# Token sums from stored halves, on GpSimd, during attention; rows of y in places of their own; second halves of weights at new paces

## The chip, the cores and the metric

The kernel runs on one core of a Trainium2 chip, in one launch. The time is the device time of that core in microseconds (us). The kernel before took a median of 1056.4 us over three runs (1053.79 to 1057.5).

## The reference

What is computed is random-feature attention, a gated feed-forward layer, and a second feed-forward layer with a cosine gate, all in fp32:

```python
q_p, k_p = phi(q_s), phi(k_s)             # exp features, 128 of them
kv = np.einsum('bhsm,bhsd->bhmd', k_p, v)
num = np.einsum('bhsm,bhmd->bhsd', q_p, kv)
den = np.einsum('bhsm,bhm->bhs', q_p, k_p.sum(axis=2))[..., None] + 1e-06
x = (num / den), as 2304 tokens x 512
# layer 1: 512 -> 1536 -> 512
xn = x / rms * rms_g
g = xn @ w_gate
x = (g / (1 + exp(-g)) * (xn @ w_val)) @ w_out
# layer 2: 512 -> 2048 -> 512
h = x @ w_in
out = (h * np.cos(h)) @ w_out2
```

4 batches, 8 heads, 576 positions, head size 64. The weights arrive as float64.

## The kernel before, in words

**Tiling.** The 2304 tokens are 18 tiles of 128, or 6 blocks of 384; two blocks that follow each other are a pair, so there are 3 pairs. The 1536 hidden features of layer 1 are 12 chunks in three groups of four, the 2048 of layer 2 are 16 chunks in groups of 6, 5 and 5. Every fp32 operand of a matmul is kept as a high and a low half of type fp32r, and a product is three matmul passes (high x high, low x high, high x low).

**Weights.** The class `Weights` turns each 128x512 chunk of float64 into fp32 on the device: that is its front (`front`: four VectorE instructions on lines 165, 167, 169 and 174, one ScalarE scaling on L159, one GpSimd add on L177). The result goes to DRAM (`keep`, tensors `kept`), comes back later (`ask`, tile `b`), and is split in two halves (`split`: a ScalarE cast on L182 and a GpSimd subtraction on L185): that is its back, the second half of its way. The first 12 chunks are split straight after their front. Fronts and backs are generators: `pace` takes so many steps of each at a rate that `rate` and `rate_back` work out from the steps left, and `get` runs them at once where a product needs a chunk that isn't there. In `ask` (L203) a back that finds its chunk not yet stored runs fronts on the spot until it is.

**Attention and the first group.** 24 slots project keys and the first six query tiles. Then 48 half steps run the first group of layer 1 (gate and value product of one chunk for one block: tile `gv_ps`, 12 matmuls; output product into `y_ps`) with the steps of the twelve query tiles that remain woven in: per tile, a projection, exponentials, two transposes, the sums, the root mean square (`root`, L443 and L444 on GpSimd), the scaling (`norm`, L448 on VectorE), a transpose on TensorE (`turn`, L458, tile `xT_ps`) and the split into `xhl`. A block's halves are stored to `x_dram` when done.

**Pairs.** Groups two and three of layer 1 use a scheme with seven block products for a pair instead of eight. It needs combinations of the two blocks' token sums, T1 to T4, made once per pair by the generator `combinations` from the halves still in SBUF: 8 sums on VectorE (L561), 16 subtractions on GpSimd (L565), 8 casts on ScalarE (L569), and their stores. `job` steps it during the half steps; for the third pair what is left is run with `job(99)` in the last half step. `bring` loads operands for a pair (tiles `B` and `T`, 768 KB each). In the stretch of pairs `duo` makes the seven products (tiles X and Y, line 986, with ScalarE copies on L1011 and VectorE additions on L1014 to L1029), `ys` the output product (L1065). `unit` is the beat there: every six or so matmuls it runs what is due, one flushed job, and paced steps of weights. Partial sums of y are kept in `y_dram`; `ask(g, blk, e)` loads one row of 192 KB again and `add_y` adds to it.

**Layer 2.** `hidden` and `h_cos` make a step (12 matmuls `h_ps`, then ScalarE and VectorE), `out2` the output product two steps later (36 matmuls `o_ps`).

**What sets the order.** Each engine works its instructions in the order in which the program makes them, and SyncE (SP) issues nearly all transfers in its own such order: a transfer that waits holds back all behind it. TensorE's instructions are the same, in the same order, before and after the change.

## Time and profile before

| | |
|---|---|
| median of 3 runs | 1056.4 us |
| profiled execution: time, span | 1059.7 us, 1057.9 us |
| TensorE matmuls, busy | 990.3 us (94%) |
| VectorE, busy | 726.8 us (69%) |
| ScalarE, busy | 520.2 us (49%) |
| GpSimd, busy | 331.2 us (31%) |
| DMA queue of SP, share of 16 engines | 49.0% |

Busy time is an average over stretches that differ: attention with the first group (up to 331 us), the pairs (331 to 655 us) and layer 2 (to the end, where TensorE has no gap worth naming). TensorE is the engine that everything ends on, so what counts is where it stood idle and what it waited for, and where its clock was granted at the lower of its two levels after such a wait.

### The profile page before, as it was taken

The page shows a single profiled execution, that of the slowest core. Times are in us where ns is not written, and L with a number is a line of the kernel's source. Part 1 is how long each engine was busy: PE and PEld are TensorE (multiplying, and loading weights), DVE is VectorE, ACT ScalarE, POOL GpSimd, SP SyncE. Part 2 cuts the span into 40 slices and gives each one's busy share as a digit, 9 for nine tenths or more (in the row PEclk, how much of TensorE's full clock was granted, in tenths as well). Part 3 has the DMA queues.
Part 4 walks back from the last instruction along what each step waited for, and adds up shares of the span by engine and source line. Part 5 has one row for each costly group of instructions (what it writes and reads, how often), then busy time and mean ns, then how long its engine had stood idle before and what let it go on. Part 6 is the DMA issues. An engine that isn't in the chain of part 4 may idle for free.

```text
span 1057.9 us, 16240 instructions
## 1 busy us (share of the span) xinstructions
PE 990.3 (94%) x5905; PEld 931.6 (88%) x5905; DVE 726.8 (69%) x1275; ACT 520.2 (49%) x1133; POOL 331.2 (31%) x293
## 2 busy tenths in 40 slices
PE   9999599999986899999899986999999999999998
PEld 7988589999986798999899986999999999999997
DVE  6788897788743667687677676877555676656555
ACT  6777476776422524253534443545444444443442
POOL 2143456246255543375824274121100111000000
PEclk9999889999998899999999998999999999999999
DMA  8554464645477487846898787433301223103401
GB/s 292 151 167 164 138 209 161 209 164 178 148 255 275 149 338 250 316 123 217 297 329 301 263 288 260 158 132 128 140 1 64 96 90 129 60 1 117 152 31 60
DMA packets 75295, 185.15 MB, mean 175 GB/s; under 512 B 8016, under 2 KB 32720, under 8 KB 75216
## 3 DMA queue, kind: packets, MB, share of 16 engines
q1 hardware_dynamic: 73776, 179.34, 49.0%
q10 hardware_dynamic: 1440, 4.78, 1.3%
q8 instruction: 46, 0.75, 0.3%
q14 instruction: 33, 0.27, 0.1%
HBM read 126.94 MB, written 57.15 MB: 174 GB/s over the span
## 4 chain that ended last, share of the span: by engine, by line
PE 68%; DMA 13%; DVE 8%; issue 3%; POOL 3%; ACT 2%; SPq 1%; ACTq 0%; POOLq 0%; DVEq 0%
PE h_ps L738 18%; PE o_ps L731 6%; PE o_ps L732 6%; PE gv_ps L738 6%; PE o_ps L730 6%; PE X L986 5%; PE Y L986 4%; PE y_ps L802 4%; DMA b<-kept 3%; PE y L1065 3%; DMA y<-y_dram 3%; PE num_ps L420 2%; DMA kept<-f 2%; PE kv_ps L531 2%; DMA y_dram<-y 2%
## 5 line engine op out<-in xcount | busy, mean ns | idle before, releaser
L738 PE MATMUL h_ps<-yhl,w 128*128 128x384 f32 x1152 | 217.2, 337 | 0.0
L738 PEld LDWEIGHTS h_ps<-yhl,w 128*128 128x128 f32 x1152 | 204.9, 188 | 8.2
L177 POOL TENSOR_TENSOR f<-f,raw 128x512 f32<-128x512 f32 x68 | 94.3, 1387 | 258.9 <-DVE raw L174 231.0
L185 POOL TENSOR_TENSOR w<-b,w 128x512 fp32r<-128x512 f32 x72 | 96.5, 1347 | 186.4 <-ACT w L182 101.4
L730 PE MATMUL o_ps<-w,o 128*128 128x512 f32 x288 | 112.8, 392 | 9.3 <-ACT o L827 9.3
L732 PE MATMUL o_ps<-w,o 128*128 128x512 f32 x288 | 114.6, 398 | 0.0
L731 PE MATMUL o_ps<-w,o 128*128 128x512 f32 x288 | 114.4, 397 | 0.0
L824 ACT ACTIVATE turns<-turns,half_pi 128x384 f32<-128x384 f32 x96 | 59.2, 617 | 108.6 <-DVE turns L819 108.6
L1065 PE MATMUL y<-t,w 128*128 128x384 f32 x576 | 104.5, 341 | 7.0 <-ACT t L994 7.0
L738 PE MATMUL gv_ps<-xhl,w 128*128 128x384 f32 x576 | 109.2, 338 | 0.8 <-DVE eT L410 0.4
L1065 PEld LDWEIGHTS y<-t,w 128*128 128x128 f32 x576 | 102.8, 193 | 7.7 <-ACT t L994 7.7
L738 PEld LDWEIGHTS gv_ps<-xhl,w 128*128 128x128 f32 x576 | 101.8, 190 | 1.6 <-DVE eT L410 1.0
L986 PE MATMUL X<-T,w 128*128 128x384 f32 x432 | 83.6, 341 | 10.7 <-ACT r L1011 8.7
L829 DVE TENSOR_TENSOR o<-turns,o 128x384 fp32r<-128x384 f32 x96 | 55.1, 574 | 51.8 <-ACT o L827 51.2
L986 PEld LDWEIGHTS X<-T,w 128*128 128x128 f32 x432 | 76.8, 192 | 12.1 <-ACT r L1011 9.8
L826 DVE TENSOR_TENSOR turns<-h_ps,turns 128x384 f32<-128x384 f32 x96 | 53.4, 556 | 46.8 <-ACT turns L824 46.3
L827 ACT CAST o<-turns 128x384 fp32r<-128x384 f32 x96 | 49.3, 513 | 67.9 <-DVE turns L826 67.3
L818 DVE SCALAR_TENSOR_TENSOR r<-turns,h_ps 128x384 f32<-128x384 int32 x96 | 53.1, 554 | 36.2 <-ACT turns L817 36.1
L802 PE MATMUL y_ps<-t,w 128*128 128x384 f32 x288 | 62.8, 354 | 10.9 <-ACT t L789 8.6
L817 ACT ACTIVATE turns<-h_ps,quarter 128x384 int32<-128x384 f32 x96 | 55.7, 580 | 34.4 <-PE h_ps L738 34.0
L730 PEld LDWEIGHTS o_ps<-w,o 128*128 128x128 f32 x288 | 54.5, 189 | 18.4 <-ACT o L827 9.6
L182 ACT CAST w<-b 128x512 fp32r<-128x512 f32 x72 | 42.6, 597 | 46.5 <-DMA b<-kept 36.3
(102 smaller groups left out, 1767.0 us busy)
## 6 DMA issues: line engine op xcount, KB each, us to landing
raw<-wc SPq DMA_DIRECT2D x59, 512.0 KB, 4.2
yhl<-yh_dram SPq DMA_DIRECT2D x32, 768.0 KB, 5.9
T<-T_dram SPq DMA_DIRECT2D x20, 768.0 KB, 9.3
kept<-f SPq DMA_DIRECT2D x56, 256.0 KB, 4.5
b<-kept SPq DMA_DIRECT2D x56, 256.0 KB, 3.7
B<-x_dram SPq DMA_DIRECT2D x15, 768.0 KB, 7.2
x_dram<-xhl SPq DMA_DIRECT2D x12, 768.0 KB, 6.1
y_dram<-y SPq DMA_DIRECT2D x48, 192.0 KB, 2.4
```

The costliest lines, as they stand in the source:

```text
L177: nc.gpsimd.tensor_tensor(f32(f), f32(f), rest, op=ALU.add)
L185: nc.gpsimd.tensor_tensor(t[:, 1, to], src, f32(t[:, 0, to]), op=ALU.subtract)
L730: nc.tensor.matmul(o, w[0], x[0], start=first, stop=False)
L731: nc.tensor.matmul(o, w[0], x[1], start=False, stop=False)
L732: nc.tensor.matmul(o, w[1], x[0], start=False, stop=last)
L738: nc.tensor.matmul(o, w[i], x[j], start=n == 0, stop=n == len(terms) - 1)
L802: nc.tensor.matmul(yacc[blk][e], w[:, i, e * P:(e + 1) * P], t[:, j], start=first and i + j == 0, stop=last and j == 1)
L817: nc.scalar.activation(a, h, AF.Identity, bias=quarter, scale=1.0 / (2 * math.pi))
L824: nc.scalar.activation(r, r, AF.Sin, bias=half_pi)
L829: nc.vector.tensor_tensor(o[:, 1], r, f32(o[:, 0]), op=ALU.subtract)
L986: nc.tensor.matmul(o, w[:, i, c + kk * P:c + (kk + 1) * P], x[:, j, kk], start=begin and n == 0, stop=n == 5, skip_group_check=True)
L1065: nc.tensor.matmul(acc[e], w[:, i, e * P:(e + 1) * P], t[:, j], start=f == fs[0] and i + j == 0, stop=f == fs[-1] and j == 1)
```

## The change

Six edits go together.

1. **Token sums.** `combinations` no longer reads the halves in SBUF. It loads high and low half of each operand again from `x_dram` into one tile (`ask`, four loads for each half of a pair), and makes the sums with GpSimd (L585), as it does the subtractions (L588, L597). The high halves are a GpSimd copy too (L594) for the first two pairs, a ScalarE copy (L592) for the third. High and low half stand in one tile and are stored with one transfer; they stand in reverse order, which `seventh` takes into account.
2. **The third pair's sums** move out of the first group: `limit` stops `job` after two pairs, and `unit` steps the third pair's sums during the stretch of pairs. `bring` puts off the load of a T that isn't made yet. `job(99)` is gone.
3. **Rows of y** that `put_away` stores at the end of the first group, and those that `ask` loads again, have a tag of their own with 7 buffers, where they shared four buffers with the hidden rows or had four. The rows of the second block of a pair are asked for during `duo`, all but the last. Their additions, and the store after them, come a unit or more later.
4. **Fronts** load two chunks ahead from within the front instead of three ahead after its end. A back no longer runs fronts when its chunk isn't stored: it gives way (`BLOCKED`), unless `get` forces it. The tile `b` has four buffers, and the chunk after next is asked for earlier.
5. **Paces.** 32 chunks (before: 25) have their front by the end of the first group, 54 (before: 56) by the start of layer 2. Backs don't start before six fronts are done, then run at 1.0 or 1.3 steps a unit among pairs. The last fronts are spread over 52 steps of layer 2 instead of 32.
6. **Room.** One buffer of weights less in the first ring (20), two in the second; fewer buffers for loads and features of attention once the keys are done.

```diff
         def ask(self, c):
-            if c < len(self.todo) and c not in self.b:
-                while c not in self.kept:
-                    next(self.fronts)
-                b = self.b[c] = conv.tile([P, 512], F32, tag="b", name=f"b{c}", bufs=3)
+            if c in self.kept and c not in self.b:
+                b = self.b[c] = conv.tile([P, 512], F32, tag="b", name=f"b{c}", bufs=4)
                 nc.sync.dma_start(b, self.kept[c])
...
         def back(self, c):
+            while c not in self.kept:
+                if not self.forced:
+                    yield BLOCKED
+                else:
+                    next(self.fronts)
+                    self.n_front += 1
             self.ask(c)
             self.ask(c + 1)
...
             g, v = self.b.pop(c - 1), self.b.pop(c)
+            self.ask(c + 2)
...
-        jobs = []
+        jobs, combined, limit = [], set(), [NPAIR - 1]
...
-            def total(x, kk, name):
-                r = tp.tile([P, NB], F32, tag="r", name=f"{name}_{p}_{kk}")
-                nc.vector.tensor_tensor(r, f32(x[:, 0, kk]), f32(x[:, 1, kk]), op=ALU.add)
-                return r
+            def ask(b, i, kk):
+                a = tp[0].tile([P, 2, NB], F32, tag="s", name=f"s{p}_{b}_{i}_{kk}", bufs=tp[1])
+                nc.sync.dma_start(a, in_dram[2 * p + b][i][:, :, kk])
+                return a
+
+            def total(a):
+                nc.gpsimd.tensor_tensor(a[:, 0], a[:, 0], a[:, 1], op=ALU.add)
...
+            def high(a):
+                if few:
+                    nc.scalar.copy(a[:, 1].bitcast(F32R), a[:, 0])
+                else:
+                    nc.gpsimd.tensor_copy(a[:, 1].bitcast(F32R), a[:, 0])
...
-            y = row(F32, f"y{blk}_{e}")
+            y = row(F32, f"y{blk}_{e}") if not more else more[0].tile([P, NB], F32, tag="y", name=f"y{blk}_{e}", bufs=YROWS)
...
         def bring(g, p, name):
+            if name[0] == "T" and p not in combined:
+                at(1, bring, g, p, name)
+                return
...
+        FRONTS_BY_1, FRONTS_BY_2 = 32, 54
...
-            rates = wts.rate(2 * C1 * G + 1, N1 - n) / 2, 1.0 if tail else wts.rate_back(C1 * G + 6, N1 - G - n) / 2
+            back = 2.0 if tail else wts.rate_back(C1 * G + 5, N1 - G - n) / 2
+            if wts.n_front < 6 * FRONT:
+                back = 0.0
+            rates = wts.rate(FRONTS_BY_1, N1 - G + 1 - n) / 2 if n <= N1 - G else 0.0, back
...
-            if n == N1 - 1:
-                job(99)
...
-            wts.pace(*tempo)
+            wts.pace(tempo[0] if clock[0] >= 30 else 0.0, 1.3 if clock[0] % (3 * UNITS) >= 100 or clock[0] % (3 * UNITS) < 16 else 1.0)
+            job(2 if clock[0] % 5 < 2 else 1)
...
                     if i < KD:
                         at(3, ask, g, 2 * p, i)
+                    elif i < 7:
+                        at(3, ask, g, 2 * p + 1, i - KD)
...
-            for e in range(KD):
-                at(3 + e, ask, g, 2 * p + 1, e)
+            at(6, ask, g, 2 * p + 1, 3)
```

VectorE in the fifth half step of the first group: `qmx7` belongs to query tile 7, `x5` is the row of tile 5 that `turn` waits for; `f12` to `f15` and `raw12` to `raw14` are fronts of weights. Before:

```order
L391 TENSOR_REDUCE qmx7_1_1579<-qp_ps7_1_1562 128x4
L174 SCALAR_TENSOR_TENSOR raw11_1315<-raw11_1315 128x512
L165 TENSOR_SCALAR f12_1598<-W12_1519 128x512
L167 SCALAR_TENSOR_TENSOR f12_1598<-W12_1519,f12_1598 128x512
L169 TENSOR_SCALAR raw12_1409<-f12_1598 128x512
L174 SCALAR_TENSOR_TENSOR raw12_1409<-raw12_1409 128x512
...
L165 TENSOR_SCALAR f15_1638<-W15_1632 128x512
L167 SCALAR_TENSOR_TENSOR f15_1638<-W15_1632,f15_1638 128x512
L448 SCALAR_TENSOR_TENSOR x5_1433<-x5_1433,ms5_1488,gain_255 128x512
L788 TENSOR_TENSOR gv0_2_1538<-gv_ps0_2_1_1646,gv0_2_1538 128x384
```

Now, in the same place:

```order
L399 TENSOR_REDUCE qmx7_1_1572<-qp_ps7_1_1555 128x4
L169 SCALAR_TENSOR_TENSOR f11_1508<-W11_1457,f11_1508 128x512
L171 TENSOR_SCALAR raw11_1315<-f11_1508 128x512
L456 SCALAR_TENSOR_TENSOR x5_1430<-x5_1430,ms5_1484,gain_255 128x512
L838 TENSOR_TENSOR gv0_2_1531<-gv_ps0_2_1_1590,gv0_2_1531 128x384
```

Fifteen instructions of fronts stood between the two rows of attention; now there are two.

GpSimd in half steps 26 to 28 of the first group: `b11` to `b22` (before) and `s1` (now) are the sums of the second pair, `ms14` is the root mean square of query tile 14. Before:

```order
L443 TENSOR_SCALAR ms13_2851<-ms13_2851 128x1
L444 TENSOR_TENSOR ms13_2851<-ms13_2851,minus_half_76 128x1
L565 TENSOR_TENSOR b21_1_0_2955<-b21_1_0_2955,b22_1_0_2824 128x384
L565 TENSOR_TENSOR b22_1_0_2824<-b22_1_0_2824,T2h_1_0_2946 128x384
L565 TENSOR_TENSOR b21_1_0_2955<-b21_1_0_2955,T4h_1_0_3012 128x384
L565 TENSOR_TENSOR b11_1_1_3072<-b12_1_1_3074,b11_1_1_3072 128x384
L443 TENSOR_SCALAR ms14_3048<-ms14_3048 128x1
```

Now:

```order
L588 TENSOR_TENSOR s1_1_0_0_2786<-s1_1_1_0_2796,s1_1_0_0_2786 128x384
L588 TENSOR_TENSOR s1_1_1_0_2796<-s1_1_1_0_2796,s1_0_0_0_2784 128x384
L594 CAST s1_0_0_0_2784<-s1_0_0_0_2784 128x384
L597 TENSOR_TENSOR s1_0_0_0_2784<-s1_0_0_0_2784 128x384
L594 CAST s1_1_0_0_2786<-s1_1_0_0_2786 128x384
L597 TENSOR_TENSOR s1_1_0_0_2786<-s1_1_0_0_2786 128x384
L183 TENSOR_TENSOR f23_2984<-f23_2984,raw23_2789 128x512
L191 TENSOR_TENSOR w14_2990<-b13_2470,w14_2990 128x512
L585 TENSOR_TENSOR s1_0_1_0_2831<-s1_0_1_0_2831 128x384
L588 TENSOR_TENSOR s1_0_1_0_2831<-s1_0_1_0_2831,s1_1_1_0_2796 128x384
L594 CAST s1_1_1_0_2796<-s1_1_1_0_2796 128x384
L451 TENSOR_SCALAR ms14_3021<-ms14_3021 128x1
```

Between the roots of tiles 13 and 14 stood four GpSimd instructions; now there are sixteen, of which these are the last eleven.

SP where the operands of the third pair come in (T1_1_2 to T4_1_2), now; before, each stood between single rows of y, without a store of T ahead:

```order
L1103 DMA y1_3_2_4820<-y_dram3_2_3435 128x384
L600 DMA T2_dram2_3954<-s2_1_1_1_4449 256x1x384
L600 DMA T4_dram2_3956<-s2_0_1_1_4672 256x1x384
L966 DMA T4_1_2_4847<-T4_dram2_3956 128x1536
L966 DMA T3_1_2_4849<-T3_dram2_3955 128x1536
L966 DMA T1_1_2_4851<-T1_dram2_3953 128x1536
L966 DMA T2_1_2_4853<-T2_dram2_3954 128x1536
```

The four loads follow the last stores of the sums at once, and T2, the first of them that TensorE uses, is the last in the queue.

## Rows read from the trace of the kernel before

**Rows 1.** Waits of PE: line, releaser: us in total, times, longest

```profile
PE xT_ps L458 <- DVE x L448: 11.8, 1, 11.8
PE o_ps L730 <- ACT o L827: 9.3, 1, 9.3
PE X L986 <- ACT r L1011: 8.7, 3, 4.7
PE y_ps L802 <- ACT t L789: 8.6, 1, 8.6
PE y L1065 <- ACT t L994: 7.0, 2, 3.9
PE Y L986 <- DVE r L1014: 4.9, 7, 2.0
PE y_ps L802 <- ACT y L768: 2.4, 1, 2.4
```

**Rows 2.** Windows: length, busy PE, PEld, DVE, ACT, POOL; PEclk, DMA share, GB/s

```profile
133.00:138.00 5.00, 4.75 (x20) 4.78 (x21) 4.35 (x8) 4.37 (x9) 2.09 (x2) 0.53 0.71 213
324.00:329.00 5.00, 4.54 (x14) 4.54 (x15) 1.16 (x2) 2.31 (x5) 4.36 (x5) 0.51 0.42 153
350.00:357.00 7.00, 6.20 (x21) 6.20 (x22) 2.62 (x5) 3.17 (x7) 2.74 (x3) 0.56 0.52 181
526.00:531.00 5.00, 4.85 (x19) 4.85 (x20) 2.71 (x3) 1.96 (x5) 4.49 (x5) 0.66 1.04 409
655.00:661.00 6.00, 5.13 (x16) 4.26 (x17) 4.70 (x10) 2.82 (x6) 1.29 (x1) 0.59 0.60 202
```

**Rows 3.** Timeline of VectorE: start, us, instruction [idle before, releaser]

```profile
121.57 1.65 DVE L167 SCALAR_TENSOR_TENSOR f<-W,f 128x512 int32<-128x512 int32 x1
...
132.35 0.75 DVE L448 SCALAR_TENSOR_TENSOR x<-x,ms,gain 128x512 f32<-128x512 f32 x1
```

**Rows 4.** Timeline of ScalarE, 112 to 140 us

```profile
130.02 0.62 ACT L182 CAST w<-b 128x512 fp32r<-128x512 f32 x1 [6.04 <-DMA b<-kept]
```

**Rows 5.** Timeline of GpSimd, 112 to 140 us

```profile
121.28 1.39 POOL L177 TENSOR_TENSOR f<-f,raw 128x512 f32<-128x512 f32 x1 [0.63 <-DVE raw L174]
```

**Rows 6.** Waits of all engines, 300 to 360 us

```profile
DVE b L561 <- DMA T_dram<-b: 15.0, 4, 5.4
...
ACT y L768 <- DMA y_dram<-y: 7.7, 1, 7.7
```

**Rows 7.** Groups of GpSimd by form: count | busy us, mean ns | idle before

```profile
L177 POOL TENSOR_TENSOR f<-f,raw 128x512 f32<-128x512 f32 x68 | 94.3, 1387 | 258.9 <-DVE raw L174 231.0 <-issue 26.1 <-DMA raw<-wc 1.9
L185 POOL TENSOR_TENSOR w<-b,w 128x512 fp32r<-128x512 f32 x64 | 89.7, 1406 | 186.4 <-ACT w L182 101.4 <-PE h_ps L738 80.4 <-DMA b<-kept 4.5
...
L565 POOL TENSOR_TENSOR b<-b,b 128x384 f32<-128x384 f32 x24 | 27.0, 1124 | 36.9 <-DVE b L561 30.0 <-DMA T_dram<-b 5.2 <-POOL b L565 1.1
```

**Rows 8.** Windows, half steps 24 to 39 of the first group

```profile
224.00:292.00 68.00, 67.68 (x456) 66.08 (x455) 56.10 (x104) 43.08 (x102) 34.29 (x35) 1.00 0.47 159
```

**Rows 9.** Groups of VectorE by form, 150 to 310 us

```profile
L561 DVE TENSOR_TENSOR b<-xhl 128x384 f32<-128x384 f32 x20 | 14.0, 714 | 6.2 <-DMA T_dram<-b 6.2
...
L167 DVE SCALAR_TENSOR_TENSOR f<-W,f 128x512 int32<-128x512 int32 x9 | 8.1, 897 | 0.1
...
L169 DVE TENSOR_SCALAR raw<-f 128x512 int32<-128x512 int32 x10 | 5.4, 537 | 0.1
```

**Rows 10.** Waits of SP's queue, 300 to 660 us

```profile
SPq L153 <- POOL f L177: 64.9, 19, 7.8
SPq L205 <- POOL w L185: 46.5, 24, 7.9
```

**Rows 11.** Waits of VectorE, 300 to 660 us

```profile
DVE y L1042 <- DMA y<-y_dram: 18.5, 10, 5.6
```

**Rows 12.** DMA issues, 330 to 650 us: count, KB each, median us to landing

```profile
T<-T_dram SPq DMA_DIRECT2D x18, 768.0 KB, 9.6
```

**Rows 13.** Timeline of TensorE among the pairs, 332 to 342 us

```profile
336.99 2.24 PE L986 MATMUL X<-T,w 128*128 128x384 f32 x12
```

More of the change, by code (lines that the diff above doesn't have):

```diff
@@ L276, in early_back @@
             for i in self.split(self.f.pop(c), self.todo[c]):
-                if c + 3 not in self.raw:
-                    self.load(c + 3)
+                self.load(c + 3)
                 yield
@@ L285, in all_fronts @@
             for c in range(self.fused, len(self.todo)):
-                steps = self.front(c)
-                next(steps)
-                yield
-                next(steps)
-                if c - 1 in self.f:
-                    self.keep(c - 1)
-                yield
-                for _ in steps:
-                    yield
-                self.load(c + 3)
+                yield from self.front(c)
+            yield
+            yield
             self.keep(c)
@@ L504, in attention_then_ffn, with att_tile @@
         ap = early.enter_context(tc.tile_pool(name="att", bufs=2, side="right", reuse_waits="tile"))
-        depth = {"gain": 1, "raw": 4, "feat": 5, "mx": 6, "den": 4}
+        depth = {"gain": 1, "raw": 3, "feat": 3, "mx": 6, "den": 4}
+        with_keys = {"raw": 1, "feat": 2}
+        turn_of = {"raw": 0, "feat": 0}
+        keys = [True]
+        def att_tile(what, shape, dt, name):
+            own = depth.get(what, 2)
+            if keys[0] and what in with_keys:
+                n = turn_of[what] % (own + with_keys[what])
+                turn_of[what] += 1
+                if n >= own:
+                    return vp.tile(shape, dt, tag=what, name=name, bufs=with_keys[what])
+            return ap.tile(shape, dt, tag=what, name=name, bufs=own)
         kv = [ap.tile([P, KVW], F32, name=f"kv{b}", bufs=1) for b in range(B)]
@@ L510, in attention_then_ffn @@
         vt = [vp.tile([P, H + 1, D], F32, name=f"v{i}", bufs=1) for i in range(NV)]
-        att = Attention(
-            lambda what, shape, dt, name: ap.tile(shape, dt, tag=what, name=name, bufs=depth.get(what, 2)), "q", kv)
+        att = Attention(att_tile, "q", kv)
         acc = {}
@@ L592, in combinations @@
+                yield from [None] * (3 if few else 1)
+                high(s1)
                 yield
[L593 to L594 removed]
+                if few:
+                    high(s2)
+                    yield from [None] * 4
+                lower(s1)
                 yield
[L596 to L597 removed]
+                if not few:
+                    high(s2)
+                    yield
+                lower(s2)
@@ L617, in query_step @@
+                lower(s4)
+                keep("T2", kk, s3)
+                yield from [None] * 2
+                keep("T4", kk, s4)
+                yield
         def query_step(t, s):
@@ L664, in attention_then_ffn @@
             todo.sort(key=lambda e: e[0])
-        AHEAD = 3
+        AHEAD = [3]
         order = sorted(tiles)
+        asked = set()
         def load_ahead(s):
             at = order.index(s) if s in tiles else -1
-            if at >= 0 and at + AHEAD < len(order):
-                att.load(*tiles[order[at + AHEAD]])
+            if at >= 0 and at + AHEAD[0] < len(order) and at + AHEAD[0] not in asked:
+                asked.add(at + AHEAD[0])
+                att.load(*tiles[order[at + AHEAD[0]]])
         def older(s, *steps):
@@ L932, in attention_then_ffn @@
             older(s, 1, 0)
-            job(3 if tail else 2)
+            job(3)
             wts.pace(*rates)
-            job(2)
-            if n == N1 - 1:
-                job(99)
-                for name in NAMES[2:4]:
-                    bring(1, 0, name)
+            job(3)
+            if n > N1 - G and early_names:
+                bring(1, 0, early_names.pop(0))
             flush(3)
@@ L955, in attention_then_ffn @@
                 assert s + 2 > max(then)
+                while len(combined) < 2:
+                    job(1)
+                combine.close()
                 open_between()
-                bring(1, 0, "B11")
-                bring(1, 0, "B21")
-        for name in NAMES[4:]:
+                early_names = ["B11", "B21", "T2", "T1", "T4"]
+            if n >= N1 - G and early_names:
+                bring(1, 0, early_names.pop(0))
+        for name in NAMES[4:6]:
             bring(1, 0, name)
-        sp.close()
+        limit[0] = NPAIR
+        tp[:] = [combine.enter_context(tc.tile_pool(name="combinations2", bufs=3, reuse_waits="tile")), 3]
         clock, due = [0], {}
```

145 lines of the change are left out of this document (82 added, 63 removed).

## The prediction

> **What bounds the kernel now.** I read the waits of TensorE first, then the granted clock after them, then for each wait the timeline or the waits of the engine that it names. TensorE's instructions don't change, so the time moves only by its waits and by what it works at the lower clock behind them. The reader is to see five places.
>
> A, 121 to 138 us: 11.8 us for one scaling on VectorE [rows 1].
> B, 301 to 329 us, end of the first group: 8.6 us for t and 2.4 us for a row of y [rows 1].
> C, 339 to 357 us, first pair: 8.7 us for the copies L1011 [rows 1].
> D, later pairs: 7.0 us for t and 4.9 us in seven pieces for L1014 [rows 1].
> E, 646 to 661 us, start of layer 2: 9.3 us for o [rows 1].
>
> After long waits the granted clock sits near 0.5, the lower level; what that costs is PE's busy time in the stretch by what the clock lacks to 1.00 [rows 2]: A 4.75 x 0.47 = 2.2, B 4.54 x 0.49 = 2.2, C 6.20 x 0.44 = 2.7, D 4.85 x 0.34 = 1.6 and E 5.13 x 0.41 = 2.1 us. With it: A 14.0, B 13.2, C 11.4, D 13.5, E 11.4, together 63.5 us. That is nearly all that can be won; the rest of TensorE's time is work.
>
> **The change part by part: what goes.**
>
> A. The scaling stood behind fifteen instructions of fronts, which the first back ran on the spot because its chunk wasn't stored; among them ScalarE waited 6.04 us for that chunk's way to DRAM and back [rows 4], and the scaling came at 132.35 [rows 3]. Now two stand there, and backs start only after six fronts. The whole 14.0 us goes.
>
> B. In these half steps the third pair's sums are run, with `job(99)` in the last; VectorE waits 15.0 us for stores of T to free its rows, with the gated product behind it in its queue [rows 6]. The sums leave this stretch, and nothing heavy comes in: the fronts end before it. 13.2 us go.
>
> C. ScalarE waits 7.7 us for y's stores to free one of the four shared rows [rows 6], and the copies that release TensorE's X stand behind it. With seven rows of its own y waits for nothing. 11.4 us go. What is late next is the T3 load, issued after the last product of the group; several products stand ahead of its use, so I put it at nothing, at most 2 us.
>
> D. SP stands 64.9 us in loads of raw weights that wait for a front's GpSimd addition, and 46.5 us in loads of b that wait for a back's [rows 10]; what is queued behind comes late, and VectorE waits 18.5 us for rows of y [rows 11]. The earlier load of raw, the fourth b and the earlier asks take these waits from SP's head. But ScalarE's casts of weights stay in line ahead of t's, and two transfers of T more for the third pair come in. From nothing to all of the 13.5 us can go; I take half, 6.7.
>
> E. Three of the last four rows of y now come a product earlier, but the fourth is still asked for one unit ahead, and casts, additions and splits of y still stand between the first h and its o on ScalarE and VectorE. Of the 11.4 us I leave 2.5, about four pieces of 0.6 us that TensorE doesn't cover (an estimate); 8.9 go.
>
> Sum of what goes: 14.0 + 13.2 + 11.4 + 6.7 + 8.9 = 54.2 us.
>
> **What comes in.** GpSimd's sums are the price. Half steps 24 to 39 are the fullest place: VectorE 56.1 and GpSimd 34.3 of 68.0 us, TensorE without a gap [rows 8]. In the order I count there, now against before: GpSimd's work for sums 32 instructions against 16, of fronts 9 against 5, of backs 6 against 4. That adds 16 x 1.12 + 4 x 1.39 + 2 x 1.41 = 26.3 us [rows 7], so GpSimd has 60.6 of 68.0. VectorE loses 8 sums of 0.71 and gets 35 instructions of fronts against 18; with 0.7 us each, between 0.54 and 0.90 [rows 9], that is +17 x 0.7 - 8 x 0.71 = +6.2, so 62.3 of 68.0. Both still fit on average, neither does in pieces: sixteen GpSimd instructions now stand between two roots, 13 x 1.12 + 2 x 1.39 + 1.41 = 18.7 us of work for three half steps of 68 / 16 = 4.25 us, and `root` of tile 14 stands at their end. Its scaling and its transpose on TensorE wait behind it; the other query tiles on VectorE wait behind the scaling. Cover is the half step between `root` and `turn`.
>
> The two engines also hold each other up: L167 took 1.65 us at 121.57 [rows 3], beginning inside an addition of GpSimd that ran from 121.28 for 1.39 us [rows 5], where its mean is 0.90 [rows 9]. If nothing could overlap, VectorE's 55 instructions there that touch SBUF alone, at about 0.55 us undisturbed (an estimate from the 0.54 of L169 and the 0.71 of L561), would need 30 us beside GpSimd's 60.6: 22 us too much. If they overlapped freely it would cost nothing, and the light last eight half steps take up some of any lag. So between 0 and 22 us; the nearest row is the stretch before, where the same sum is 34.3 + 46 x 0.55 = 59.6 of 68 without a wait, so I take 8, nearer the low end, with the first pair's sums (half steps 9 to 18) in it. The Trainium skill, "SBUF — State Buffer", section "SBUF: two separate sides", says the port pair that VectorE and GpSimd share is an exclusive lock held for a whole instruction, the loser blocking fully. The pair of rows at 121 us agrees with it; by that rule alone the 22 us would stand, and it is my first rival.
>
> The GpSimd copy of L594 has no row. It reads one operand where the subtraction reads two, so I price it like that, 1.12; the ends are 0 and the dearest row, 1.41 [rows 7], worth -18 to +5 us of GpSimd's time over 16 copies, most of it hidden.
>
> The third pair's T: the four loads follow the last stores, T2 last. 84 matmuls of TensorE's order stand between their issue and T2's first use, 84 / 12 x 2.24 = 15.7 us [rows 13]. A load of T takes 9.6 us in the median [rows 12], the first must wait for its store, and four compete: between 0 and 6 us of stall, I take 2. If that wait comes, four other loads and the rows of y behind them in SP's queue come late as well.
>
> The paces in layer 2 I cost at nothing: TensorE has no gap there, VectorE's and GpSimd's fronts get thinner, and a back is cast a full step ahead of its use. If one came late, a cast and a subtraction of about 2 us would show.
>
> Sum: -54.2 + 8 + 2 = -44.2 us. The profiled execution took 1059.7 us (span 1057.9 and 1.8 around it), so 1015.5 on its scale; it lies 3.3 above the median of 1056.4, so I forecast 1056.4 - 44.2 = 1012 us.
>
> **Rivals.**
>
> The lock holds fully, and VectorE with GpSimd bounds attention: 22 instead of 8 us, with some lower clock behind it: 1012 + 14 to 20, about 1029 us. For it: the two rows at 121 us. Against: half steps 24 to 39 ran without a gap at 59.6 of 68.
>
> The pairs stay bound by transfers: D's 13.5 stays whole, T2 costs 6, E keeps 6: 1012 + 6.8 + 4 + 3.5, about 1026 us. For it: loads of 9.6 us [rows 12], and the third pair's stores and loads are added. Against: SP's head is freed of 111 us of waits [rows 10].
>
> All covers hold: nothing of D and E is left and attention takes the sums without a wait: 1012 - 6.8 - 2.5 - 8, about 995 us. Against: the order's sixteen GpSimd instructions in a row.
>
> Slower: the queue of GpSimd in attention. 64 instructions of sums for two pairs stand ahead of twelve roots; each 0.1 us that one costs beyond 1.12 lengthens that queue by 6.4 us. From 1.12 + 44/64 = 1.8 us each it decides, and the kernel is no faster; at 2.0 it comes to 1012 + 64 x 0.88 = 1068 us. For it: the price of L594 and of operands read in strided halves isn't shown. Against: no two-input row of GpSimd is above 1.41 [rows 7].
>
> **How the numbers follow.** Chances: forecast (1000 to 1022) 0.46, the lock 0.20, transfers 0.13, all covers 0.10, slower 0.11, of which about 0.03 end within 0.3% of before (some 3 us, what a measurement of this kernel can't tell from no change). So faster 0.89, same 0.03, slower 0.08. The range reaches from the case in which all covers hold to somewhat beyond the two dearer ones, 996 to 1044; the forecast's own range is 1000 to 1022.
>
> **What would show it.** Right: no wait of TensorE for the scaling near 121 us, none for t in the last half steps of the first group, none for L1011 in the first pair, and SP's waits on GpSimd shrunk. The new price shows as waits for the scaling between 145 and 290 us, with GpSimd above 0.85 busy, and as one wait of X or Y for a load of T in the third pair. Wrong it would be if VectorE's instructions of fronts grow well beyond 0.9 us in attention, if the copies L594 take more than 1.5 us, or if TensorE's waits at A, B or C stand there under another name.

## The result, and the profile after

The changed kernel took a median of 1007.24 us (1006.58 to 1008.9), the kernel before 1056.68 beside it: a ratio of 0.9539, 95% interval 0.9517 to 0.9561. Forecast were 1012 us, between 996 and 1044. The profiled execution spans 1007.1 us against 1057.9.

TensorE's order is the same in all kernels here, so the start of the same matmul can be laid side by side. The table gives the us from one such start to the next, taken from TensorE's rows of each trace: the first matmul of half step 8, then half steps 8 to 23, 24 to 39 and 40 to 47 of the first group, the pairs, and from the first h (638 us before, 596 after) to the last matmul's end (layer 2). The experiments' rows are used further down. Where kernels don't differ, half steps 8 to 23 still vary (82.1 to 84.2); the other columns repeat within 0.8.

| kernel | to 8 | 8-23 | 24-39 | 40-47 | pair 1 | pair 2 | pair 3 | pairs 4-6 | layer 2 |
|---|---|---|---|---|---|---|---|---|---|
| before | 144.1 | 79.8 | 68.4 | 38.5 | 61.7 | 48.7 | 45.8 | 151.2 | 415.3 |
| after | 130.5 | 84.2 | 72.5 | 25.1 | 47.8 | 45.8 | 54.5 | 135.2 | 407.7 |
| undo_backs_wait | 141.2 | 84.5 | 70.9 | 25.0 | 47.8 | 46.6 | 49.5 | 135.2 | 407.1 |
| undo_place_of_sums | 131.0 | 82.2 | 72.5 | 25.1 | 80.0 | 45.8 | 45.8 | 135.2 | 407.6 |
| undo_rows_of_y | 130.8 | 82.1 | 72.5 | 25.1 | 54.4 | 46.2 | 50.8 | 135.2 | 407.7 |
| undo_heads | 130.5 | 87.6 | 72.5 | 29.2 | 47.8 | 47.4 | 52.9 | 135.7 | 408.9 |
| undo_paces | 130.3 | 82.6 | 73.6 | 25.0 | 51.4 | 47.4 | 46.9 | 137.8 | 405.9 |
| undo_paces_and_heads | 131.0 | 86.3 | 75.3 | 26.3 | 53.8 | 47.3 | 47.9 | 141.0 | 409.2 |
| first_b_early | 130.6 | 79.8 | 72.5 | 25.1 | 47.8 | 46.3 | 52.5 | 135.2 | 407.6 |
| copies_on_scalar | 130.9 | 83.0 | 70.7 | 25.0 | 47.8 | 46.6 | 54.1 | 135.2 | 407.7 |
| no_sums_in_attention | 130.9 | 78.5 | 68.6 | 25.0 | 47.8 | 45.8 | 55.1 | 135.2 | 407.6 |
| third_pair_faster | 130.8 | 83.7 | 72.6 | 25.1 | 50.1 | 55.6 | 45.8 | 135.2 | 408.4 |
| best1 | 130.9 | 79.0 | 70.7 | 25.0 | 47.8 | 46.6 | 51.7 | 135.2 | 407.6 |
| best2 | 130.9 | 79.1 | 70.9 | 25.0 | 47.8 | 46.7 | 51.2 | 135.2 | 408.1 |

A pair in which TensorE never waits takes 45.8 us, the last one 43.7 (its last 12 output matmuls stand behind the first h), and the first 47.8 (it has 12 output matmuls of the first group in it). Before, the pairs had 32.7 us beyond that; after, 8.7, all in the third.

The waits of TensorE after [rows 1], longest first (line and releaser: us in total, times, longest):

```profile
PE X L1051 <- DMA T<-T_dram: 6.2, 1, 6.2
PE o_ps L779 <- ACT o L877: 2.9, 2, 2.5
PE num_ps L428 <- DVE eT L418: 2.6, 1, 2.6
```

Of the seven groups of before only the one for o is left, at 2.9 instead of 9.3 us. The windows (length, busy PE, PEld, DVE, ACT and POOL, then PEclk, DMA share, GB/s) stand at A, B and C, which were slow [rows 2], at the stretch that is slow now, at E, and over half steps 24 to 39 as they lie after the change:

```profile
119.00:124.00 5.00, 5.00 (x35) 4.96 (x35) 2.70 (x5) 2.45 (x6) 1.80 (x2) 1.00 0.04 7
307.00:312.00 5.00, 5.00 (x31) 5.00 (x30) 0.79 (x2) 0.79 (x2) 2.16 (x2) 1.00 0.65 265
323.00:330.00 7.00, 7.00 (x43) 7.00 (x42) 4.57 (x8) 3.35 (x7) 6.05 (x7) 1.00 0.42 127
414.00:421.00 7.00, 4.57 (x14) 4.60 (x15) 0.00 (x0) 2.34 (x5) 0.00 (x0) 0.55 0.57 202
606.00:612.00 6.00, 4.98 (x23) 3.96 (x23) 5.06 (x10) 3.49 (x8) 1.28 (x1) 1.00 0.80 275
214.70:287.20 72.50, 69.73 (x458) 66.71 (x457) 64.61 (x112) 43.05 (x99) 56.44 (x56) 1.00 0.71 245
```

At A, B and C TensorE is full at 1.00 where the clock sat near 0.5 before; at E the clock is at 1.00 too. The slow place is new, 414 to 421 us. In the last row, the half steps of [rows 8], VectorE is busy 64.6 us (62.3 were forecast) and GpSimd 56.4 (60.6), and TensorE is idle 2.8 of 72.5 us, where before it was idle 0.3 of 68.

**The wait for T2.** Timeline after (start, us, instruction, idle before and releaser):

```profile
399.32 1.68 SPq L600 DMA_DIRECT2D T_dram<-s  x2
...
403.26 2.12 SPq L966 DMA_DIRECT2D T<-T_dram  x4
...
408.02 2.25 PE L1051 MATMUL Y<-B,w 128*128 128x384 f32 x12
...
416.43 1.94 PE L1051 MATMUL X<-T,w 128*128 128x384 f32 x5 [6.17 <-DMA T<-T_dram]
```

SP issued four loads of T at once, T2 the last of them, and TensorE was at T2 by 410.26: 7.0 us after the first issue. The 84 matmuls of the prediction are counted right, but from the place of the issue in the order; SP came to it late, because the stores on L600 ahead of it waited for GpSimd.

**The wait at 192 us**, which the prediction did not have:

```profile
186.55 0.52 SPq L600 DMA_DIRECT2D T_dram<-s  x1
187.78 1.21 SPq L209 DMA_DIRECT2D b<-kept  x2
...
191.93 0.62 ACT L188 CAST w<-b 128x512 fp32r<-128x512 f32 x1 [5.62 <-DMA b<-kept]
192.99 1.32 DVE L840 TENSOR_TENSOR t<-gv,t 128x384 fp32r<-128x384 f32 x1 [3.65 <-ACT t L839]
...
194.24 0.68 DVE L418 COPY eT<-eT_ps 128x512 f32<-128x512 f32 x1
...
194.97 2.69 PE L428 MATMUL num_ps<-kv,eT 128*128 128x128 f32 x16 [2.63 <-DVE eT L418]
```

Read it upwards: TensorE waits for VectorE's copy, which stands behind t, which stands behind ScalarE's cast of the very first b, whose load SP issued 4 us before, behind a store of T.

**SP and GpSimd.** SP's waits after, from 300 to 660 us as in [rows 10] (64 us of it are layer 2 now, 22 were before), and GpSimd's forms in attention (count, busy us, mean ns, idle before) [rows 7]:

```profile
SPq L155 <- POOL f L183: 38.1, 10, 8.8
SPq L209 <- POOL w L191: 21.3, 13, 8.1
SPq L600 <- POOL s L597: 19.9, 6, 6.6
```

```profile
L597 POOL TENSOR_TENSOR s<-s 128x384 fp32r<-128x384 f32 x16 | 18.6, 1161 | 1.1
L588 POOL TENSOR_TENSOR s<-s,s 128x384 f32<-128x384 f32 x16 | 18.5, 1154 | 1.1
L585 POOL TENSOR_TENSOR s<-s 128x384 f32<-128x384 f32 x16 | 18.0, 1130 | 1.3 <-DMA s<-x_dram 1.2
L594 POOL CAST s<-s 128x384 fp32r<-128x384 f32 x16 | 11.5, 722 | 0.0
```

The three with two operands took 1.13 to 1.16 us (1.12 was used); the copy L594, which had no row, 0.72 instead of 1.12: 16 x 0.40 = 6.4 us less GpSimd time than was counted.

### The profile page after: what moved, and what is told of

It reads as the page before. It is cut to its first block, busy times and chain, and to the rows that moved or that the text cites. A ratio compares the mean times of both kernels' runs of the same rounds, so it can differ in the third digit from the quotient of the medians.

```text
span 1007.1 us, 16187 instructions
## 1 busy us (share of the span) xinstructions
PE 980.4 (97%) x5905; PEld 924.3 (92%) x5905; DVE 724.2 (72%) x1251; ACT 512.8 (51%) x1117; POOL 371.4 (37%) x333
## 3 DMA queue, kind: packets, MB, share of 16 engines
q1 hardware_dynamic: 79920, 188.78, 53.8%
## 4 chain that ended last, share of the span: by engine, by line
PE 75%; DVE 8%; POOL 5%; DMA 4%; issue 3%; ACT 3%; SPq 1%; ACTq 0%; POOLq 0%; DVEq 0%
PE h_ps L787 19%; PE X L1051 9%; PE y L1130 8%; PE Y L1051 7%; PE o_ps L781 7%; PE o_ps L780 7%; PE o_ps L779 6%; PE gv_ps L787 4%; PE kv_ps L551 2%; PE y_ps L852 2%; PE num_ps L428 1%; DMA T<-T_dram 1%; POOL s L588 1%; POOL s L585 1%; PE kp_ps L390 1%
## 5 line engine op out<-in xcount | busy, mean ns | idle before, releaser
L183 POOL TENSOR_TENSOR f<-f,raw 128x512 f32<-128x512 f32 x68 | 95.5, 1405 | 281.6 <-DVE raw L178 250.4
L1130 PE MATMUL y<-t,w 128*128 128x384 f32 x576 | 101.0, 334 | 0.0
L1130 PEld LDWEIGHTS y<-t,w 128*128 128x128 f32 x576 | 99.9, 188 | 0.0
L1051 PE MATMUL X<-T,w 128*128 128x384 f32 x432 | 82.6, 340 | 6.2 <-DMA T<-T_dram 6.2
L869 DVE SCALAR_TENSOR_TENSOR turns<-turns,r 128x384 f32<-128x384 int32 x96 | 64.9, 676 | 3.3
L169 DVE SCALAR_TENSOR_TENSOR f<-W,f 128x512 int32<-128x512 int32 x68 | 64.7, 952 | 1.0
L779 PEld LDWEIGHTS o_ps<-w,o 128*128 128x128 f32 x288 | 54.1, 188 | 12.1 <-ACT o L877 3.6
```

Source lines behind the costliest of these rows:

```text
L169: nc.vector.scalar_tensor_tensor(f, w, SIGN, f, op0=ALU.bitwise_and, op1=ALU.bitwise_or)
L183: nc.gpsimd.tensor_tensor(f32(f), f32(f), rest, op=ALU.add)
L779: nc.tensor.matmul(o, w[0], x[0], start=first, stop=False)
L869: nc.vector.scalar_tensor_tensor(f32(a), a, -TWO_PI_LO, b, op0=ALU.mult, op1=ALU.add)
L1051: nc.tensor.matmul(o, w[:, i, c + kk * P:c + (kk + 1) * P], x[:, j, kk], start=begin and n == 0, stop=n == 5, skip_group_check=True)
L1130: nc.tensor.matmul(acc[e], w[:, i, e * P:(e + 1) * P], t[:, j], start=f == fs[0] and i + j == 0, stop=f == fs[-1] and j == 1)
```

## The experiments

Each was timed beside the kernel before; ratios are to it, with their interval, and the changed kernel's own is 0.9539.

**Place A.** Fronts run on the spot again:

```diff
             while c not in self.kept:
-                if not self.forced:
-                    yield BLOCKED
-                else:
-                    next(self.fronts)
-                    self.n_front += 1
+                next(self.fronts)
+                self.n_front += 1
...
-            if wts.n_front < 6 * FRONT:
-                back = 0.0
```

> The changed kernel, but backs run the missing fronts on the spot again and are not held until six chunks have their fronts. My theory (the 14.0 us of place A went because nothing stands ahead of the scaling any more): TensorE waits some 10 us or more for the scaling's transpose near 121 us again, and the kernel takes 1007 + 13.6 = about 1021 us. Rival (the gain came from elsewhere, such as the load of raw weights that now goes out earlier in each front): the forced fronts find their data at once, the wait stays under 4 us and the time within 4 us of 1007.

0.9614 (0.958 to 0.9647). ScalarE and TensorE in that kernel's timelines (of TensorE's two waits of 3.6 and 3.75 us, at 127.85 and 135.34, the second):

```profile
132.86 0.62 ACT L188 CAST w<-b 128x512 fp32r<-128x512 f32 x1 [6.10 <-DMA b<-kept]
```

```profile
135.34 3.63 PE L425 MATMUL num_ps<-kv,eT 128*128 128x128 f32 x16 [3.75 <-ACT gv L830]
```

The cast waits 6.1 us for its chunk, as it did before [rows 4], and half step 8 begins 10.7 us later. TensorE's wait stands under other names than the scaling's, since the order around it moved. The end is later by only 0.0075 x 1056.5 = 7.9 us: the third pair gives 5.0 back, where TensorE, coming later, waits 3.5 instead of 6.2 us for T2.

**Place B.** The third pair's sums in the first group again, still on GpSimd:

```diff
                 early_names = ["B11", "B21", "T2", "T1", "T4"]
+                limit[0] = NPAIR
+                tp[:] = [combine.enter_context(tc.tile_pool(name="combinations2", bufs=3, ...)), 3]
+            while n == N1 - 1 and jobs:
+                job(1)
...
-        limit[0] = NPAIR
-        tp[:] = [combine.enter_context(tc.tile_pool(name="combinations2", bufs=3, ...)), 3]
```

> The changed kernel, but the third pair's sums stand in the last half steps of the first group again, what is left of them all at once in the last one; they stay on GpSimd. My theory (place B went because the sums left this stretch): the wait for t and y before the pairs comes back with about 13 us, the wait of 6.2 us for T2 at 410 us goes with its 3 us of low clock; 1007 + 13 - 9 = about 1011 us. Rival (what went was the waiting of VectorE's additions, which stood in one queue with the gated products; on GpSimd the place does no harm): no wait at B, the wait for T2 is gone, about 998 us.

0.9777 (0.9746 to 0.9807), 25 us slower than the changed kernel; the first pair takes 80.0 us. TensorE, and what ScalarE waits for from 310 to 350 us:

```profile
345.84 4.21 PE L1053 MATMUL X<-T,w 128*128 128x384 f32 x12 [28.68 <-ACT r L1078]
```

```profile
ACT s L592 <- POOL s L588: 31.4, 6, 9.4
```

Each theory is half right. T2's wait is gone (pair 3 at 45.8), but half steps 40 to 47 stay at 25.1: with the sums in their old place, but on GpSimd, no wait comes back at B itself. A wait of 28.7 us comes in the first pair instead: ScalarE's casts of s wait for the sums, the sums wait for their halves (15.2 us of loads in the same window, three buffers), and the copies of X stand behind the casts. So the sums could not stay there in this form. That B's own wait came from VectorE's additions, as [rows 6] has it, fits both kernels, but no run puts the additions back on VectorE.

**Place C.** y from the four shared rows:

```diff
-            y = row(F32, f"y{blk}_{e}") if not more else more[0].tile([P, NB], F32, tag="y", ...)
+            y = row(F32, f"y{blk}_{e}")
```

> The changed kernel, but the first group's y goes to DRAM from the four shared rows again. My theory (place C): ScalarE's copies of y wait some 8 us for stores, TensorE waits about 9 us for the copies of X behind them in the first pair, 1007 + 11 = about 1018 us. Rival (the first pair starts 18 us earlier and SP's queue is freer, so stores land in time): under 3 us, about 1009 us.

0.9583 (0.955 to 0.9615). ScalarE in that kernel from 305 to 365 us, and TensorE:

```profile
ACT r L1076 <- DMA y_dram<-y: 6.8, 2, 4.7
```

```profile
327.04 2.29 PE L1051 MATMUL X<-T,w 128*128 128x384 f32 x6 [4.27 <-ACT r L1076]
```

The time lies between theory and rival; its interval touches the changed kernel's. The mechanism is C's, in the same place, and about half as dear: pair 1 loses 6.6 us, pair 3 gives 3.7 back. The first pair's 13.9 us were thus not the rows' alone; the paces (below) hold another part.

**Place D**, in three kernels. The heads of SP's queue:

```diff
-            if not self.early:
-                self.load(c + 2)
...
-                b = ... name=f"b{c}", bufs=4)
+                b = ... name=f"b{c}", bufs=3)
...
             g, v = self.b.pop(c - 1), self.b.pop(c)
-            self.ask(c + 2)
...
             self.out[1, f, "S4"] = (four, 256 * (f % 2))
             yield
+            self.ask(c + 2)
...
                 yield from self.front(c)
+                self.load(c + 3)
```

> The changed kernel, but loads of raw weights go out at the end of a front for the chunk three on, b has three buffers, and the b after next is asked for at the end of a back. The pairs gained 24.0 us, of which 11.4 are C's. My theory (waits at the head of SP's queue were all of the rest): SP's waits on GpSimd grow back to some 100 us in the pairs, and 15 us come back there, about 1022 us. Rival, as the prediction had it (half of it from the heads, the rest from the cast of weights and transfers): 5 to 8 us, about 1014 us. Third: nothing, 1007 us, if the waits at SP's head were off the path.

0.9615 (0.9582 to 0.9647). The 8 us are there, as the rival had it, but not where it had them: half steps 8 to 23 and 40 to 47 lose 3.4 and 4.1 us, the pairs 0.5 us in all (pairs 2 and 4 to 6 lose 2.1, the third gives 1.6 back). Then the paces:

```diff
-FRONT, BACK, BACK_OF_PAIR = 6, 4, 11
+FRONT, BACK, BACK_OF_PAIR = 6, 2, 11
...
                 next(steps)
-                yield
                 self.ask(c + 2)
                 yield
                 next(steps)
-                yield
                 yield
...
-            wts.pace(tempo[0] if clock[0] >= 30 else 0.0, 1.3 if ... else 1.0)
+            wts.pace(tempo[0], 1.0)
...
-            left = UNITS * (len(pairs) - k) - (30 if k == 0 else 0)
+            left = UNITS * (len(pairs) - k)
```

> The changed kernel with the paces of before in the pairs: a back of one chunk has two steps and not four, one step of a back in every unit, and fronts from the first unit on. Undoing the waits at the head of SP's queue cost the pairs under 1 us, so D's gain has another cause. My theory now: before, backs ran ahead of their loads, ScalarE's cast of weights waited 27.6 us in 13 pieces for b, and t's cast behind it released TensorE late; slower steps give the load its time. Then those waits grow to 15 us or more and 5 to 12 us of waits of TensorE for t and Y come back in the pairs, 1012 to 1019 us. Rival (the fourth b and the earlier asks alone are enough, whatever the pace): ScalarE's waits for b stay under 8 us and the pairs lose under 2 us, 1007 to 1009 us.

0.9555 (0.9529 to 0.9581), which is within the error of the changed kernel: pairs 1, 2 and 4 lose 3.6, 1.6 and 2.6 us, and the third gives 7.6 back, its wait for T2 being hidden by them (0.9 us of 6.2 are left). ScalarE's waits for b grew as the theory had it (16.1 us, below), TensorE's for t came back in part, and the time is the rival's. Both at once:

> Both edits undone at once: the paces, and the loads, asks and three buffers of b. Theory of two covers (either of them alone gives b's load its time): ScalarE's waits for b reach 20 us or more in the pairs, TensorE waits for t and Y as before, and D's 11.9 us of waits with their low clock come back beside the 7 us that the asks alone cost in attention: 1024 to 1032 us. Rival (D's gain lies in neither, but in y's seven rows and their earlier asks): the pairs lose under 3 us beyond what the paces alone cost, about 1015 to 1018 us.

0.9712 (0.9687 to 0.9737), 1024.5 us, 18 us over the changed kernel. In the profiled executions, 14.8 us apart, the pairs hold 6.6 of it and half steps 8 to 47 hold 6.1, so that the time came out at the theory's edge with less of D than it had. One row of ScalarE's waits from pair 2 to the start of layer 2 tells most: how long its cast of weights stood for the load of b, in the kernel before, after, with the heads undone, the paces undone, and both undone:

```profile
ACT w L182 <- DMA b<-kept: 27.6, 13, 5.0
```

```profile
ACT w L188 <- DMA b<-kept: 3.8, 2, 2.3
```

```profile
ACT w L186 <- DMA b<-kept: 13.2, 5, 4.5
```

```profile
ACT w L188 <- DMA b<-kept: 16.1, 9, 4.1
```

```profile
ACT w L186 <- DMA b<-kept: 20.9, 10, 4.8
```

With both undone TensorE waits for t again, as before [rows 1]; its waits from 372 to 609 us:

```profile
PE y L1127 <- ACT t L1056: 3.6, 2, 2.4
```

That one edit covers for the other shows in the first pair, which loses nothing with the heads undone, 3.6 us with the paces and 6.0 with both. In pairs 2 and 4 to 6 the losses nearly add up: 2.1 us over the undisturbed time for the heads, 4.2 for the paces, 7.3 for both. Before, these pairs lost 18.9. The other 11.6 are not accounted for by a run: the seven rows of y and their earlier asks in the pairs remain as a cause, and were not tried alone.

**What attention pays.** The first b asked for two fronts earlier:

```diff
             if c - 1 in self.f and c > self.fused:
                 self.keep(c - 1)
+            if c == self.fused + 3:
+                self.ask(self.fused)
```

> The changed kernel, but the first b (chunk 12) is asked for two fronts earlier, so that its load doesn't stand in the half step of its cast. My theory (half of the 8.6 us that attention lost is this one load: ScalarE's cast waited 5.6 us for it, TensorE 2.6 us behind it, then 1.4 us of low clock): the wait for eT at 192 us goes and the kernel takes 1007 - 4 = about 1003 us. Rival (GpSimd and VectorE are late there anyway, by the sums): the wait comes back behind another instruction, and the time stays within 1 us of 1007.

0.9508 (0.9481 to 0.9535), 3.3 us faster, with intervals that overlap a little. The window 185 to 200 us, after and in this kernel (columns as above):

```profile
185.00:200.00 15.00, 12.37 (x81) 11.56 (x80) 9.55 (x23) 6.43 (x12) 6.96 (x7) 0.89 0.67 224
```

```profile
185.00:200.00 15.00, 15.00 (x107) 14.72 (x106) 13.70 (x28) 8.73 (x21) 9.49 (x10) 1.00 0.72 234
```

Wait and low clock are gone; half steps 8 to 23 take 79.8 us, as before the change, 2.3 to 4.4 less than in the kernels that don't differ there. Next, the sums of the first two pairs left out:

```diff
-                nc.gpsimd.tensor_tensor(a[:, 0], a[:, 0], a[:, 1], op=ALU.add)
+                few and nc.gpsimd.tensor_tensor(a[:, 0], a[:, 0], a[:, 1], op=ALU.add)
...             # likewise in less and lower; high does nothing for these pairs
```

> The changed kernel without GpSimd's 64 instructions for the sums of the first two pairs (their loads and stores stay, so T of two pairs holds other numbers and the output is not the reference's). My theory: of the 8.6 us that attention lost, the sums cost the 4.2 us in half steps 24 to 39, and the 4.4 us before belong to the first cast of b; 1007 - 4 = about 1003 us, with the wait of 2.6 us for eT at 192 us still there. Rival (GpSimd's work and the shared port cost all of it): the wait at 192 us goes too, 1007 - 8.6 = about 998.5 us. Third (VectorE's denser fronts cost it): 1006 to 1007 us.

0.9456 (0.9429 to 0.9484), 8.8 us faster; from half step 8 to the pairs 172.1 us instead of 181.8. My theory falls and the rival holds: without the sums all of attention's price goes, most of the wait at 192 us included (it shrank to 1.0). The earlier ask removes that wait too, so it hangs on both: on the late ask, because without the sums ScalarE's cast still waits 4.7 us for its b, and on the sums, because SP held a store ahead of that b for 1.6 us until one of them was done. How the 9.7 us divide between GpSimd's own queue, the stores behind it and VectorE's longer instructions, no run separates.

How the sums get at VectorE can be read from forms of fronts (count, busy us, mean ns), after in 214 to 286 us and without the sums in 210 to 278 us, the same half steps; one instruction takes 0.2 to 0.3 us longer beside the sums:

```profile
L178 DVE SCALAR_TENSOR_TENSOR raw<-raw 128x512 f32<-128x512 uint32 x9 | 8.8, 980 | 0.1
L169 DVE SCALAR_TENSOR_TENSOR f<-W,f 128x512 int32<-128x512 int32 x8 | 8.4, 1046 | 0.2
L167 DVE TENSOR_SCALAR f<-W 128x512 int32<-128x512 int32 x8 | 6.3, 785 | 1.1 <-ACT W L161 1.1
```

```profile
L169 DVE SCALAR_TENSOR_TENSOR f<-W,f 128x512 int32<-128x512 int32 x8 | 6.5, 811 | 0.2
L178 DVE SCALAR_TENSOR_TENSOR raw<-raw 128x512 f32<-128x512 uint32 x9 | 6.2, 688 | 0.1
...
L167 DVE TENSOR_SCALAR f<-W 128x512 int32<-128x512 int32 x9 | 4.6, 506 | 1.7 <-ACT W L161 1.7
```

Last, the 16 copies of high halves on ScalarE:

```diff
-                    nc.gpsimd.tensor_copy(a[:, 1].bitcast(F32R), a[:, 0])
+                    nc.scalar.copy(a[:, 1].bitcast(F32R), a[:, 0])
```

> The changed kernel, but the 16 copies of high halves for the first two pairs stand on ScalarE. They took 0.5 to 0.7 us each on GpSimd, about 10 us of its time. My theory (GpSimd's queue between two roots, and its meeting VectorE, make the late scalings): half steps 24 to 39 get 1 to 2 us shorter, about 1005.5 us. Rival (ScalarE's exponentials are behind TensorE's next matmuls and a copy that waits for GpSimd's sum holds them up): 1008 to 1011 us.

0.9515 (0.9485 to 0.9545). Half steps 24 to 39 take 70.7 instead of 72.5 us, as expected; the timed gain, 2.5 us, is within the two intervals.

**The third pair.** Its sums at double pace:

```diff
-            job(2 if clock[0] % 5 < 2 else 1)
+            job(2)
```

> The changed kernel, but the third pair's sums advance by two steps in every unit instead of two in two of five, so that they end some 20 us earlier. My theory (the sums end too late, so the loads of T go out last and at once): the 6.2 us wait for T2 at 410 us and the 3.4 us of low clock behind it go, 1007 - 9 = about 998 us. Rival (transfers bind: loads of T take their 8 us beside the others wherever they stand): a wait of 3 us or more for a T stays, 1004 us or more.

0.9577 (0.9546 to 0.9608), 4 us slower than the changed kernel, with intervals that overlap a little. Neither theory: no T is waited for any more, but pair 2 now takes 55.6 us. TensorE's and ScalarE's waits from 362 to 418 us:

```profile
PE X L1051 <- ACT r L1076: 4.7, 1, 4.7
PE Y L1051 <- ACT r L1076: 2.7, 1, 2.7
```

```profile
ACT s L592 <- POOL s L588: 8.9, 1, 8.9
ACT s L592 <- DMA y_dram<-y: 7.8, 2, 5.4
```

The casts of s come to ScalarE's queue before their operands are ready, and the copies of X and Y stand behind them. Instead, each T loaded as soon as it is stored, with the two gains of attention:

```diff
             def keep(n, kk, a):
+                if kk:
+                    stored.add((p, n))
                 nc.sync.dma_start(to[n][:, :, kk], a)
...
-            if name[0] == "T" and p not in combined:
+            if name[0] == "T" and (p, name) not in stored:
```

> The changed kernel with the first b asked for two fronts earlier, the 16 copies of high halves on ScalarE, and each T of the third pair loaded as soon as its own second half is stored: T1 and T3 some 10 us before T2, and T2 ahead of T4's store in SP's queue. Theory (T2 came late because three other loads of 768 KB shared the DMA engines with it): the 6.2 us at 410 us and the 3.4 us of low clock shrink to under 2 us; with 3 us for the first b and 2 us for the copies about 994 us. Rival (GpSimd's sums themselves end too late, so that T2 is stored too late whatever is loaded beside it): 3 us or more of the wait stay, 1000 us or more.

0.9499 (0.947 to 0.9528). TensorE waits for no T, as the theory had it, but the third pair still takes 51.7 us, and the time is the rival's. ScalarE and TensorE in that kernel:

```profile
411.35 0.66 ACT L161 ACTIVATE W<-raw 128x512 f32<-128x512 f32 x1 [8.49 <-DMA raw<-wc]
```

```profile
412.84 2.61 PE L1055 MATMUL X<-T,w 128*128 128x384 f32 x7 [4.26 <-ACT r L1080]
```

The load of raw weights stood behind T4's, which waited in SP's queue for its own store. With T4's load five units later:

```diff
-                if kk:
+                if kk and n == "T4" and few:
+                    at(5, stored.add, (p, n))
+                elif kk:
                     stored.add((p, n))
```

> The version with the first b early, copies on ScalarE and T by name, in which only T4's load stands five units later in SP's queue. In that version the wait for T2 was gone, but 4.3 us for a copy of X came in its place at 413 us: SP stood 5.5 us at T4's load, which waited for its store, the load of raw weights behind it went out at 404.3 us, and ScalarE's first step of a front waited 8.5 us for it with the copies of X behind. Theory (one queue, SP's, sets it): with the raw load ahead of T4's load the wait for X goes and with it some 2 us of low clock; the third pair takes some 46.5 instead of 51.7 us and the kernel about 997 us. Rival (the transfers of this stretch, four T, y and raw weights, are too much for the DMA engines in any order): a wait of 3 us or more stays in the third pair, for T4 or for raw weights, about 1001 us.

1000.47 us, 0.9467 (0.9444 to 0.949): 7.6 us faster than the changed kernel, with intervals that don't meet, and the fastest here of those that make all the sums; from the version without T4's delay it is not told apart. ScalarE's wait for raw weights is down from 8.5 to 3.6 us, and one of VectorE takes its place, for a row of y whose load SP held 4.3 us, until a store of y had landed:

```profile
415.03 0.56 DVE L1113 TENSOR_TENSOR y<-y,y 128x384 f32<-128x384 f32 x1 [9.68 <-DMA y<-y_dram]
```

```profile
416.71 3.77 PE L1057 MATMUL X<-T,w 128*128 128x384 f32 x12 [3.70 <-DVE r L1089]
```

That wait was there in the changed kernel too, beside T2's; from 395 to 425 us:

```profile
DVE y L1107 <- DMA y<-y_dram: 10.3, 1, 10.3
```

ScalarE waited 8.9 us for raw weights there as well. So three loads of one stretch were late together, each hiding the next; the rival, that 3 us or more stay in any order, has the third pair's 5.4 us on its side. Whether more rows of y would end it was not tried.

## Why the prediction was right, step by step

- **A**, 14.0: 13.6 came. The cause is shown: with the fronts run on the spot 10.7 us come back, with the same cast's wait.
- **B**, 13.2: 13.4 came. The wait went, as forecast; that the sums can't stand in its place is shown, that its 13.4 us came from VectorE's share of them is read from the trace before.
- **C**, 11.4: pair 1 gained 13.9, all that it had beyond 47.8. Of the 8.7 us for L1011, 1.5 belong to the fourth pair, and 2.0 for VectorE's L1018 in the first pair were not counted. Undoing the rows gives 6.6 of the 13.9 back, both of the D edits 6.0. The wait and its place were right; it hung on more than the rows.
- **D**, "From nothing to all of the 13.5 us can go; I take half, 6.7": 18.9 went. This is the step that was furthest off. Two things were wrong. The size: pairs 2 and 4 to 6 were 18.9 us longer than undisturbed ones, which the starts of the pairs in the trace of before would have told. TensorE's waits by name were 13.2 of it; the other 5.7 stand in matmuls that ran longer behind these waits, for which one window had given 1.6. And the cover: the step leaned on SP's heads, which alone are worth 2.1 us in these pairs. It was right that the casts of weights stood ahead of t; that their slower pace in the diff would free them was not seen. With heads and paces undone 7.3 of the 18.9 come back; the cause of the rest stays open.
- **E**, 8.9: layer 2 gained 7.6, and o waits 2.9 us, near the 2.5 left. No run undid E's edits alone, so its cause is argued and not shown.
- **GpSimd in attention**, +8: 8.5 came (8-23 and 24-39 together 148.2, now 156.7), and without the sums 9.7 of 181.8 us vanish. That the size fits is in part luck: 8 was a choice between 0 and 22, and the inside was different. The signs that were named did not come: TensorE waits for no scaling, and GpSimd is busy 56.4 of 72.5 us, 0.78 and not above 0.85. About half of it was the first b; in half steps 24 to 39 TensorE waits 2.5 us in four pieces for VectorE's copies, splits and gated products, not for the scalings behind `root`.
- **T2**, +2: 8.7 came, 6.2 us of wait and the clock behind. The bounds ended at 6 because the time from issue to use was taken from the order and not from SP's waits.

Sum of the table's columns: -13.6 + 8.5 - 13.4 - 13.9 - 2.9 + 8.7 - 16.0 - 7.6 = -50.2 us where -44.2 was forecast. D and C brought 14.7 more than priced, T2 took 6.7 more, E, attention, A and B the other 2.0. So the total is nearer than its parts: D and T2 missed in opposite directions. The slower rival fell with its price: no instruction of the sums took more than 1.2 us in the mean. The transfers' rival had its term for T2 and nothing else; the rival in which all covers hold was right for D and wrong for attention.

## What to carry to other kernels

Price a pipelined stretch by the spread between equal pieces (here: pairs), not only by named waits; the fastest piece shows what all of them could take. Where an in-order transfer queue feeds a deadline, count from when the queue gets to the issue, and look at what else is late in the same stretch, because the next wait stands right behind the one removed. An edit undone alone can seem worthless when another wait shrinks by what it costs: the paces lost 7.8 us in three pairs here and got 7.6 back in the third.

## What the hardware showed

VectorE's instructions of fronts, which read and write SBUF alone, are held up by what is left of a large GpSimd instruction when they begin. In the timeline after:

```profile
270.06 1.76 POOL L183 TENSOR_TENSOR f<-f,raw 128x512 f32<-128x512 f32 x1
...
270.96 0.42 DVE L440 TENSOR_TENSOR x<-num_ps,den 128x256 f32<-128x256 f32 x1
...
276.54 1.49 POOL L183 TENSOR_TENSOR f<-f,raw 128x512 f32<-128x512 f32 x1
276.90 1.68 DVE L169 SCALAR_TENSOR_TENSOR f<-W,f 128x512 int32<-128x512 int32 x1
...
280.30 0.68 DVE L178 SCALAR_TENSOR_TENSOR raw<-raw 128x512 f32<-128x512 uint32 x1
```

L169 begins inside L183 with 276.54 + 1.49 - 276.90 = 1.13 us of it left, and lasts 1.68, that is 1.13 + 0.55; undisturbed it takes 0.69. The same sum fits L178 at 236.22, 247.72, 262.72 and 272.04 us (0.94, 0.67, 0.83 and 0.74 left; 1.49, 1.22, 1.39 and 1.29 taken). L440, which reads one operand from PSUM, is not lengthened inside L183. Nor are three instructions of fronts that begin with 0.36 to 0.47 us left of a small GpSimd one (L452, 128x1): they take 0.43, 0.69 and 0.70 us. The other way round, L183 at 270.06 begins with 0.59 us of VectorE's L456 left and takes 1.76 us, where at 217.26, with no such neighbour, it takes 1.31. From half step 8 to the pairs 34 of 77 instructions of fronts begin inside one of GpSimd's large ones with over 0.2 us left, and lose 20.8 us; without the sums it is 8 of 77 and 6.2 us. So the sums took 14.6 us of VectorE's time here; the stretch got 9.7 us shorter without them.

This is what the Trainium skill, "SBUF — State Buffer", section "SBUF: two separate sides", says for a VectorE instruction with two SBUF inputs or in a mode that uses both ports: whichever of the two starts first holds the shared pair for its whole instruction. The times of L169 and L178 agree with it; those beside L452 show no such hold, as far as GpSimd's recorded spans can be trusted at that size. The first rival took the rule rightly and priced it wrongly, at 22 us: it let no time of the two engines overlap, while over half of the instructions of fronts (43 of 77) begin when no large GpSimd instruction is running or in its last 0.2 us.
